# A tuned one-core kernel: the second projection of six of nine blocks as seven products of quarters, in a new order of steps

## The chip, the core and the metric

The kernel runs on one core of a Trainium2 chip. A core has five engines that work side by side, each through its own instructions in order: TensorE (PE in the rows, with its weight loads as PEld) multiplies matrices into PSUM, VectorE (DVE), ScalarE (ACT) and GpSimd (POOL) do elementwise work, and SyncE (SP) starts most transfers between DRAM and SBUF. DVE and ACT read PSUM; all of them read SBUF.

The metric is the device time of one execution in microseconds (us). A separate profiled execution gives the trace.

## The reference

```python
scores = (1 / sqrt(64)) * matmul(q, k.transpose(0, 1, 3, 2))       # q, k, v: (8, 8, 576, 64)
Dmat   = where(rel >= 0, gamma[:, None, None] ** rel, 0.0)         # rel = i - j, one gamma per head
x      = matmul(scores * Dmat, v).transpose(0, 2, 1, 3).reshape(4608, 512)
h      = x @ w_in                                                  # 512 -> 2048
g      = h + sin(alpha * h) ** 2 / (alpha + 1e-9)
out    = g @ w_out                                                 # 2048 -> 512
```

All inputs and the output are float32; both kernels compute with float16 operands and float32 sums in PSUM.

## The kernel before

The 4608 rows are worked in nine blocks of 512 tokens. Blocks 0 to 7 are the first 512 tokens of batches 0 to 7; block 8 gathers the last 64 tokens of all batches.

**Attention.** Each batch is computed in pieces with a running state: q, k and v are loaded and cast to f16 (line 168 with the decay factors, line 103 or 101 without), turned, and multiplied into scores (line 342). VectorE applies the decay mask while it takes them out of PSUM (line 354), PE multiplies by v (line 384), and a sum of keys times values (line 282) is carried from piece to piece (lines 311, 316, 323, 324). Between the two halves of an output stands a marker on an engine, a POOL nop or a PE drain, that orders them.

**The two projections.** For each block, `project` makes 16 units of 128 of the 2048 features: four matmuls of 512 columns into one PSUM bank `hps` (line 519). `sine` (ACT, line 527) makes the sine, `square` squares it (DVE or POOL line 538, ACT line 536), and `product` (DVE, line 543) computes `square / alpha + h` out of the bank into `gT`. With that the unit's bank is free. Then `gemm2` (line 562) multiplies `gT`, 128 tokens at a time, with `w_out`: 16 matmuls of 512 columns for each of four chunks of a block, into a bank `ops`. `finish` copies the chunk out of PSUM (lines 101, 103) and stores it in two halves (line 555).

**Weights.** `w_in` and `w_out` come in four pieces each on POOL's queue (lines 91 and 94), each piece of `w_out` holding 512 of the 2048 features.

**What sets the order.** Each engine takes its instructions in the order in which the program was written. For blocks 0 to 2 each step is written out by hand. For blocks 3 to 8 two loops write them: in block n, unit u is projected while one quarter (four matmuls) of a chunk of block n - 1 goes through `gemm2`, and the attention of batch n + 1 is put in at fixed units. After the last unit four chunks of block 8 remain, the last in two column pieces of 320 and 192, whose results leave on the queues of SP and ACT. Buffers are taken from pools of tiles, each kind with its own number of buffers, and PSUM banks by turns (`h0`, `h1`, `h2`, `m0`, `m1`, `op`).

## Time and profile before

| | us |
| --- | --- |
| time, median of three runs | 308.1 (308.0 to 308.36) |
| the profiled execution: span from first to last instruction | 309.4 |
| last matmul ends, in the trace | 305.78 |

Times in the trace are counted from the first instruction of the profiled execution. Its mean granted TensorE clock is 0.976: it is lower in the first 25 us only.

```profile
PE   6669999999999999999999999999999999999995
DVE  1596799989859888666866586576656746655600
ACT  1434983766544766675677567756774456555411
POOL 5690774589449587759149722990030000000000
```

Each row is an engine, each digit the busy share of one fortieth of the span (7.7 us) in tenths, 9 being 90% or more. PE is full from the fourth slice to the last but one. DVE is at 8 or 9 in most slices of the first third and at 5 or 6 later. POOL, which casts inputs and keeps the states, has nothing left in the last quarter.

### The profile page before, as it was taken

The page shows a single profiled execution, that of the slowest core. Times are in us where ns is not written, and L with a number is a line of the kernel's source. Part 1 is how long each engine was busy: PE and PEld are TensorE (multiplying, and loading weights), DVE is VectorE, ACT ScalarE, POOL GpSimd, SP SyncE. Part 2 cuts the span into 40 slices and gives each one's busy share as a digit, 9 for nine tenths or more (in the row PEclk, how much of TensorE's full clock was granted, in tenths as well). Part 3 has the DMA queues.
Part 4 walks back from the last instruction along what each step waited for, and adds up shares of the span by engine and source line. Part 5 has one row for each costly group of instructions (what it writes and reads, how often), then busy time and mean ns, then how long its engine had stood idle before and what let it go on. Part 6 is the DMA issues. An engine that isn't in the chain of part 4 may idle for free.

```text
span 309.4 us, 7922 instructions
## 1 busy us (share of the span) xinstructions
PE 296.4 (96%) x3257; PEld 150.9 (49%) x3257; DVE 207.4 (67%) x298; ACT 180.7 (58%) x286; POOL 138.4 (45%) x154
## 2 busy tenths in 40 slices
PE   6669999999999999999999999999999999999995
PEld 4546555554544544454445444544454454444443
DVE  1596799989859888666866586576656746655600
ACT  1434983766544766675677567756774456555411
POOL 5690774589449587759149722990030000000000
PEclk9776999999999999999999999999999999999999
DMA  7999999699497788987788788885431111111132
GB/s 227 335 215 217 278 260 247 160 247 303 90 289 213 88 190 183 272 140 171 161 226 209 179 163 192 230 199 132 101 72 39 34 36 36 35 34 37 42 89 73
DMA packets 115540, 49.84 MB, mean 161 GB/s; under 512 B 69792, under 2 KB 111024, under 8 KB 115504
## 3 DMA queue, kind: packets, MB, share of 16 engines
q1 hardware_dynamic: 110912, 44.97, 60.0%
q0 software_dynamic: 4224, 4.19, 8.1%
q8 instruction: 25, 0.41, 0.6%
q10 hardware_dynamic: 368, 0.18, 0.3%
q14 instruction: 11, 0.09, 0.1%
HBM read 36.74 MB, written 9.44 MB: 149 GB/s over the span
## 4 chain that ended last, share of the span: by engine, by line
PE 84%; DMA 3%; POOL 3%; SPq 3%; DVE 2%; ACT 1%; issue 1%; DVEq 0%; ACTq 0%; POOLq 0%
PE ops L562 39%; PE hps L519 37%; DMA q<-in_q_dram 3%; PE o L384 3%; PE sc L342 2%; SPq L115 2%; POOL q L168 1%; PE kv L282 1%; DVE s L316 1%; DVE ret L354 1%; PE o L406 1%; SPq L120 1%; ACT s_t L527 1%; POOL k L168 1%; PE tr L201 0%
## 5 line engine op out<-in xcount | busy, mean ns | idle before, releaser
L562 PE MATMUL ops<-w_out,gT 128*128 128x512 f16 (+2 forms) x592 | 142.4, 374 | 0.3 <-ACT kvs L101 0.2
L543 DVE SCALAR_TENSOR_TENSOR gT<-ss_t,inva,hps 128x512 f16<-128x512 f16 x144 | 106.2, 745 | 53.1 <-ACT ss_t L536 46.1
L527 ACT ACTIVATE s_t<-hps,alpha_t 128x512 f16<-128x512 f32 x144 | 97.1, 686 | 71.3 <-PE hps L519 68.8
L519 PE MATMUL hps<-xT,w_in 128*128 128x512 f16 (+1 forms) x544 | 127.7, 370 | 0.0
L519 PEld LDWEIGHTS <-w_in 128*128 128x128 f16 x608 | 59.1, 99 | 64.5 <-issue 0.9
L562 PEld LDWEIGHTS <-gT 128*128 128x128 f16 x592 | 56.2, 98 | 64.3 <-issue 0.7
L538 DVE TENSOR_TENSOR ss_t<-s_t 128x512 f16<-128x512 f16 x72 | 42.2, 587 | 19.5 <-ACT s_t L527 18.8
L536 ACT ACTIVATE ss_t<-s_t 128x512 f16<-128x512 f16 x62 | 38.8, 631 | 0.9
L354 DVE TENSOR_TENSOR ret<-sc,mask 128x1024 f16<-128x1024 f32 (+1 forms) x32 | 35.1, 1118 | 1.9 <-PE sc L342 1.8
L168 POOL TENSOR_TENSOR k<-k,cn 128x1024 f16<-128x1024 f32 (+1 forms) x13 | 22.1, 1699 | 25.0 <-DMA k<-in_k_dram 20.7
L101 ACT COPY osb<-ops 128x512 f32<-128x512 f32 (+1 forms) x34 | 19.7, 582 | 22.0 <-PE ops L562 20.6
L168 POOL TENSOR_TENSOR q<-q,cn 128x1024 f16<-128x1024 f32 (+1 forms) x16 | 27.2, 1708 | 10.1 <-DMA q<-in_q_dram 10.0
L538 POOL TENSOR_TENSOR ss_t<-s_t 128x512 f16<-128x512 f16 x10 | 10.8, 1083 | 19.5 <-ACT s_t L527 10.7
L101 ACT CAST xT<-o 128x1024 f16<-128x1024 f32 (+1 forms) x14 | 13.2, 958 | 7.9 <-PE o L406 7.8
L324 POOL TENSOR_TENSOR kvs<-s,kvs 128x256 f32<-128x256 f32 x22 | 16.1, 730 | 3.1 <-ACT kvs L101 1.4
L103 POOL CAST v<-v 128x1024 f16<-128x1024 f32 (+1 forms) x10 | 12.2, 1234 | 9.5 <-DMA v<-in_v_dram 8.4
L519 PE MATMUL hps<-xS,w_in 128*128 128x512 f16 x64 | 16.4, 379 | 0.0
L323 POOL TENSOR_TENSOR s<-kvs,cn 128x256 f32<-128x256 f32 x22 | 14.3, 651 | 0.3
L152 POOL TENSOR_TENSOR ks<-ks,cn 128x512 f16<-128x512 f32 x4 | 4.2, 1041 | 22.0 <-PE o L384 22.0
L384 PE MATMUL o<-ret,v 64*64 64x128 f16 (+1 forms) x512 | 11.9, 226 | 1.3 <-DVE ret L354 0.7
L342 PE MATMUL sc<-qT,kT 64*64 64x128 f16 (+1 forms) x512 | 10.9, 221 | 1.9 <-DVE ret L354 1.9
L316 POOL TENSOR_TENSOR s<-kvs,cn 128x256 f16<-128x256 f32 x19 | 12.2, 646 | 1.1 <-ACT kvs L101 0.5
(59 smaller groups left out, 142.3 us busy)
## 6 DMA issues: line engine op xcount, KB each, us to landing
out_dram<-osb SPq DMA_DIRECT2D x70, 128.0 KB, 2.4
q<-in_q_dram SPq DMA_DIRECT2D x16, 512.0 KB, 6.2
k<-in_k_dram SPq DMA_DIRECT2D x10, 512.0 KB, 8.2
v<-in_v_dram SPq DMA_DIRECT2D x10, 512.0 KB, 6.2
k<-in_k_dram SPq DMA_DIRECT2D x24, 128.0 KB, 3.1
v<-in_v_dram SPq DMA_DIRECT2D x24, 128.0 KB, 3.2
w_in<-in_moe_w_in_dram POOLq DMA_DIRECT2D x4, 512.0 KB, 11.3
w_out<-in_moe_w_out_dram POOLq DMA_DIRECT2D x4, 512.0 KB, 9.8
```

Of the source, the lines that this page charges most:

```text
L101: eng.copy(d_, s_)
L168: eng.tensor_tensor(dst[:, a0:a1].rearrange("p a r t d -> p t (a r) d"), t_.rearrange("p (t a) x -> p t a x", t=2)[:, :, a0:a1].rearrange( ...
L324: nc.gpsimd.tensor_tensor(self.kvs[:, c], s32, self.kvs[:, c], ADD)
L342: matmul(sc[halves(g), t, c : c + n], kT[halves(t), 2 * a + r, halves(g)], qT[halves(t), 2 * a : 2 * a + 2, 64 * g + i0 : 64 * g + 64], st ...
L354: nc.vector.tensor_tensor(ret.rearrange("p t (z x) -> p (t z) x", z=2)[:, :, 0:n], sc.rearrange("p t (z x) -> p (t z) x", z=2)[:, :, 0:n], ...
L384: made.append(matmul(o[t][halves(e), c : c + 128].rearrange("p (r i) -> p r i", r=2)[:, :, i0:64], v16[halves(g), 4 * t + 2 * x + e, r, :] ...
L519: matmul(hps_of[n, fc][0][:, cols], w_in16[:, a, fc * P : (fc + 1) * P], xs[n][:, a, cols], start=(a == 0 and part != 1), stop=(a == KT - ...
L527: nc.scalar.activation(s_t, hps, mybir.ActivationFunctionType.Sin, bias=0.0, scale=alpha_t[:, fc : fc + 1],)
L536: nc.scalar.activation(ss_t, s_t, mybir.ActivationFunctionType.Square)
L538: eng.tensor_tensor(ss_t, s_t, s_t, MULT)
L543: nc.vector.scalar_tensor_tensor(gT[n][:, fc, :], ss_t, inva[:, fc : fc + 1], hps, MULT, ADD)
L562: matmul(ops[n, c, cols.start][:, cols], gT[n][:, fk, c * P : (c + 1) * P], w_out16[:, fk, cols], start=(fk == 0), stop=(fk == FC - 1), sk ...
```

## The change

Blocks 0, 1 and 2 keep their second projection. For blocks 3 to 8 it is computed in another way. The result of a block, 512 tokens by 512 columns, is a product of `g` (512 by 2048) and `w_out` (2048 by 512). Cut both into quarters, `g` into halves of the tokens and of the features (A11, A12, A21, A22), `w_out` into halves of the features and of the columns (B11 to B22). Four quarters of the result are then sums of eight products of quarters. The change gets them from seven (the scheme of Winograd):

- four differences of the weights, made once (`TT`, line 844): T1 = B12 - B11, T2 = B22 - T1, T3 = B22 - B12 (in place of B12), T4 = B21 - T2, in eight pieces of 128 x 1024 elements;
- four sums of `g` in every block (`SM`, line 856): S1 = A21 + A22 (in place of A21), S2 = S1 - A11, S3 = A11 - A21, S4 = A12 - S2 (in place of A12), in two pieces each, 30 of the 48 pieces on DVE and 18 on POOL;
- seven products (`PP`, line 873), each of 8 units x 2 token halves, 16 matmuls of 256 columns, 112 for a block where 64 of 512 columns were; they add up in three banks, X (P1, then P6, P7, P4), Y (P2) and Z (P5, then P3);
- the banks are copied out in between (`CP`, 17 times on ACT and 7 on DVE) and added to what was copied before (`AD`, line 889, 18 times, on DVE);
- each quarter of the result is stored with two transfers from SP's queue (`OQ`, lines 894 and 895).

A piece covers 512 features, as a transfer of `w_out` does: the first of T1 reads the first quarter of `w_out`, the second the second, and the pieces of T2 to T4 the third or the fourth. T3 is made after the last use of the old B12 by block 2.

The hand-written sequence and the loops are replaced by a table `STEPS` of all steps in order, with the number of the buffer or bank that a step takes. Blocks 0 and 1 have the old order, with the pieces of T1, T2 and T4 put in; from block 2 on the order is new, block by block overlapping. Squares move as well: DVE 43 (72 before), ACT 74 (62), POOL 27 (10). The buffers are shared: 16 f32 tiles of 128 x 1024 (`r4`), 28 f16 of 128 x 1024 (`h2`), 16 f16 of 128 x 512 (`s1`), two for `g` and eight banks, any step taking a free one.

```diff
-        for n in range(3, NBLK):
...
-                    gemm2(n - 1, u, "op")
-                    finish(n - 1, u // 4)
...
-        for c in range(3):
-            tag = next(h)
-            for u in range(4 * c, 4 * c + 4):
-                gemm2(NBLK - 1, u, tag)
-            finish(NBLK - 1, c)
-        for cols, eng in ((slice(0, 320), A_), (slice(320, 512), V)):
-            tag = next(h)
-            for u in range(12, 16):
-                gemm2(NBLK - 1, u, tag, cols)
-            finish(NBLK - 1, 3, eng, cols, (nc.sync, nc.scalar))
+STEPS = """
...
+PR.0.7.2 hps.0.7=7; ST.0.3:G; SI.0.6 s.0.6=9; WO.2; TT.1.0:V T1=0; SQ.0.11:A ss.0.11=10; SI.0.7 s.0.7=11
...
+OQ.7.21; PP.8.7.1; PP.7.3.3; CP.8.7:A u3.8=27; PP.8.5.0; AD.7.12; PP.8.4.0; AD.8.22; PP.8.4.1; OQ.7.12; PP.8.4.3
+SM.8.4.1:V; PP.8.4.2; PP.8.3.3; OQ.8.22; CP.8.4:V c21.8=2; PP.8.3.1; PP.8.3.2; PP.8.3.0; OQ.8.21; AD.8.12; OQ.8.12
+"""
...
+    def quarter_a(n, t, f, i, m):
+        return g_of(n)[:, 8 * f + i : 8 * f + i + m, 256 * t : 256 * t + 256]
+    def quarter_b(f, d, i, m):
+        return w_out16[:, 8 * f + i : 8 * f + i + m, 256 * d : 256 * d + 256]
+    def of_units(x, i, m):
+        return x.rearrange("p (u n) -> p u n", n=256)[:, i : i + m]
+    def TT(t, i, eng):
+        i *= 4
+        T = {x: of_units(big16(f"T{x}"), i, 4) for x in (1, 2, 4) if f"T{x}" in place}
+        T[3] = quarter_b(0, 1, i, 4)
+        a, b = {
+            1: lambda: (quarter_b(0, 1, i, 4), quarter_b(0, 0, i, 4)),
+            2: lambda: (quarter_b(1, 1, i, 4), T[1]),
+            3: lambda: (quarter_b(1, 1, i, 4), T[3]),
+            4: lambda: (quarter_b(1, 0, i, 4), T[2]),
+        }[t]()
+        return eng.tensor_tensor(T[t], a, b, SUB)
+    def SM(n, s, i, eng):
+        i *= 4
+        S = {x: of_units(big16(f"S{x}.{n}"), i, 4) for x in (2, 3) if f"S{x}.{n}" in place}
+        S[1], S[4] = quarter_a(n, 1, 0, i, 4), quarter_a(n, 0, 1, i, 4)
+        a, b, op = {
+            1: lambda: (S[1], quarter_a(n, 1, 1, i, 4), ADD),
+            2: lambda: (S[1], quarter_a(n, 0, 0, i, 4), SUB),
+            3: lambda: (quarter_a(n, 0, 0, i, 4), S[1], SUB),
+            4: lambda: (S[4], S[2], SUB),
+        }[s]()
+        return eng.tensor_tensor(S[s], a, b, op)
+    BANK_OF = {1: "X", 6: "X", 7: "X", 4: "X", 2: "Y", 5: "Z", 3: "Z"}
+    def PP(n, p, j):
+        ps = bank(f"{BANK_OF[p]}.{n}")
+        for u in (2 * j, 2 * j + 1):
+            left, right = {
+                1: lambda: (quarter_a(n, 0, 0, u, 1), quarter_b(0, 0, u, 1)),
+                2: lambda: (quarter_a(n, 0, 1, u, 1), quarter_b(1, 0, u, 1)),
+                3: lambda: (quarter_a(n, 0, 1, u, 1), quarter_b(1, 1, u, 1)),
+                4: lambda: (quarter_a(n, 1, 1, u, 1), of_units(big16("T4"), u, 1)),
+                5: lambda: (quarter_a(n, 1, 0, u, 1), of_units(big16("T1"), u, 1)),
+                6: lambda: (of_units(big16(f"S2.{n}"), u, 1), of_units(big16("T2"), u, 1)),
+                7: lambda: (of_units(big16(f"S3.{n}"), u, 1), quarter_b(0, 1, u, 1)),
+            }[p]()
+            for c in range(2):
+                i = matmul(
+                    ps[:, 256 * c : 256 * c + 256], left[:, 0, 128 * c : 128 * c + 128], right[:, 0, :],
+                    start=starts(f"{BANK_OF[p]}.{n}"), stop=True, skip_group_check=True,
+                )
+        return i
+    KEPT = {2: ("Y", "p2"), 6: ("X", "u2"), 7: ("X", "u3"), 4: ("X", "c21")}
+    def CP(n, p, eng):
+        b, t = KEPT[p]
+        return copy(eng, mid32(f"{t}.{n}"), bank(f"{b}.{n}"))
+    SUMS = {11: ("X", "p2"), 22: ("Z", "u3"), 12: ("Z", "u2")}
+    def AD(n, c):
+        b, t = SUMS[c]
+        return nc.vector.tensor_tensor(mid32(f"{t}.{n}"), bank(f"{b}.{n}"), mid32(f"{t}.{n}"), ADD)
+    def OQ(n, c, eng=nc.sync):
+        t = mid32(f"{dict(((11, 'p2'), (21, 'c21'), (22, 'u3'), (12, 'u2')))[c]}.{n}").rearrange("p (c d) -> p c d", c=2)
+        x = rows_of(n, 2 * (c // 10 - 1), 2)[..., 256 * (c % 10 - 1) : 256 * (c % 10)]
+        eng.dma_start(x[0], t[halves(0)])
+        return eng.dma_start(x[1], t[halves(1)])
```

In the table `:V`, `:A`, `:G` and `:P` name the engine; SQ is `square`, PD `product`, PR `project`, SI `sine`, G2 `gemm2`. The names in the rows below: `r_67` are the f32 buffers, `h_68` and `s_69` the f16 ones, `g_70` the two tiles of `g`.

The first place is on DVE, in the products of block 0's first units. Before:

```order
L543 SCALAR_TENSOR_TENSOR gT<-ss_t,inva,hps 128x512
L311 SCALAR_TENSOR_TENSOR kvs<-kvs,cn,kv 128x64 x4
L543 SCALAR_TENSOR_TENSOR gT<-ss_t,inva,hps 128x512
L538 TENSOR_TENSOR ss_t<-s_t 128x512
L543 SCALAR_TENSOR_TENSOR gT<-ss_t,inva,hps 128x512 x2
```

And of the change:

```order
L792 SCALAR_TENSOR_TENSOR g_70<-s_69,inva,banks 128x512
L532 SCALAR_TENSOR_TENSOR r_67<-r_67,cn,banks 128x64 x4
L844 TENSOR_TENSOR r_67<-w_out_65 128x1024
L792 SCALAR_TENSOR_TENSOR g_70<-s_69,inva,banks 128x512
L788 TENSOR_TENSOR s_69<-s_69 128x512
L792 SCALAR_TENSOR_TENSOR g_70<-s_69,inva,banks 128x512 x2
```

The first piece of T1, which reads the first quarter of `w_out`, now stands between the state step and the product of unit 1.

The second place is on DVE too, a little later, up to the masks of batch 1 (line 354 before, 564 now). Before:

```order
L538 TENSOR_TENSOR ss_t<-s_t 128x512 x2
L543 SCALAR_TENSOR_TENSOR gT<-ss_t,inva,hps 128x512 x4
L354 TENSOR_TENSOR ret<-sc,mask 128x1024 x2
L543 SCALAR_TENSOR_TENSOR gT<-ss_t,inva,hps 128x512
L103 COPY kT<-tr 128x512 x2
L354 TENSOR_TENSOR ret<-sc,mask 128x1024 x2
```

And of the change:

```order
L788 TENSOR_TENSOR s_69<-s_69 128x512 x2
L792 SCALAR_TENSOR_TENSOR g_70<-s_69,inva,banks 128x512
L844 TENSOR_TENSOR r_67<-w_out_65 128x1024
L792 SCALAR_TENSOR_TENSOR g_70<-s_69,inva,banks 128x512 x2
L844 TENSOR_TENSOR r_67<-w_out_65,r_67 128x1024
L792 SCALAR_TENSOR_TENSOR g_70<-s_69,inva,banks 128x512
L844 TENSOR_TENSOR r_67<-w_out_65,r_67 128x1024
L564 TENSOR_TENSOR h_68<-banks,mask 128x1024 x2
```

Three more pieces stand among the last four products of block 0, ahead of the first mask of batch 1.

The third place is the end of the program on DVE. Before:

```order
L538 TENSOR_TENSOR ss_t<-s_t 128x512
L543 SCALAR_TENSOR_TENSOR gT<-ss_t,inva,hps 128x512
L538 TENSOR_TENSOR ss_t<-s_t 128x512
L543 SCALAR_TENSOR_TENSOR gT<-ss_t,inva,hps 128x512 x2
L103 COPY osb<-ops 128x192
```

And of the change:

```order
L856 TENSOR_TENSOR r_67<-g_70 128x1024
L325 COPY h_68<-banks 128x512
L856 TENSOR_TENSOR g_70<-g_70,r_67 128x4x256
L325 COPY h_68<-banks 128x512
L889 TENSOR_TENSOR h_68<-banks,h_68 128x512 x2
L856 TENSOR_TENSOR g_70<-g_70,r_67 128x4x256
L325 COPY h_68<-banks 128x512
L889 TENSOR_TENSOR h_68<-banks,h_68 128x512
```

Where squares and products of block 8 and one copy of 192 columns stood last, there are now the sums of quarters of block 8, copies and additions; the last is an addition of 512 columns.

1643 lines of the change are left out of this document (642 added, 1001 removed).

## The prediction

> **What bounds the kernel now.** I read the busy shares on the page first, then the stretches of the run side by side, then the chain of waits.
>
> ```profile
> PE 296.4 (96%) x3257; PEld 150.9 (49%) x3257; DVE 207.4 (67%) x298; ACT 180.7 (58%) x286; POOL 138.4 (45%) x154
> PE 84%; DMA 3%; POOL 3%; SPq 3%; DVE 2%; ACT 1%; issue 1%; DVEq 0%; ACTq 0%; POOLq 0%
> ```
>
> ```profile
> 0.00:25.40 25.40, 16.74 (x328) 12.85 (x329) 14.83 (x17) 7.42 (x10) 17.51 (x29) 0.79 1.06 255
> 25.40:66.00 40.60, 40.26 (x498) 22.19 (x495) 34.83 (x60) 27.90 (x46) 22.09 (x20) 0.96 1.07 241
> 66.00:105.50 39.50, 39.31 (x580) 20.12 (x572) 33.00 (x43) 23.08 (x38) 30.13 (x34) 1.00 0.76 203
> 54.40:305.80 251.40, 250.96 (x2573) 122.01 (x2571) 167.87 (x236) 153.12 (x244) 105.26 (x109) 1.00 0.61 142
> 36.00:46.00 10.00, 9.76 (x119) 5.59 (x118) 9.61 (x16) 8.68 (x16) 7.98 (x7) 1.00 1.18 252
> 66.00:76.00 10.00, 10.00 (x105) 5.37 (x98) 9.59 (x13) 6.74 (x13) 9.69 (x14) 1.00 1.00 266
> ```
>
> Columns of the second fence: stretch, its length, then busy time of PE, PEld, DVE, ACT and POOL with their counts, granted clock, DMA share, GB/s. From 25.4 us on TensorE (PE) hardly ever stops: 40.26 of 40.60, 39.31 of 39.50, and 250.96 of 251.40 from 54.4 to its last matmul. So a us of PE work removed there is a us of time, as long as nothing else makes PE wait. The same rows say how much of the others PE tolerates: with VectorE (DVE) busy for 84 to 86% it loses 0.2 to 0.34 us in 40, and even ten-us stretches with DVE at 9.6 cost it 0 to 0.24 us.
>
> **The PE work that goes.** Blocks 3 to 8 drop 6 x 64 = 384 matmuls of 512 columns for 6 x 112 = 672 of 256.
>
> ```profile
> 120.87 1.02 PE L562 MATMUL ops<-w_out,gT 128*128 128x512 f16 x4
> 121.73 1.03 PE L519 MATMUL hps<-xT,w_in 128*128 128x512 f16 x4
> 122.60 1.03 PE L562 MATMUL ops<-w_out,gT 128*128 128x512 f16 x4
> 125.19 1.03 PE L519 MATMUL hps<-xT,w_in 128*128 128x512 f16 x4
> ```
>
> ```profile
> 54.38:55.25 0.87, 0.87 (x8) 0.78 (x8) 1.00 0.02 5
> L519 PE MATMUL hps<-xT,w_in 128*128 128x256 f16 x8 | 1.0, 273 | 0.0
> ```
>
> Durations overlap, so I take start to start: from 120.87 to 125.19 five groups of four, 4.32 us for 20, 0.216 us each. Eight of 256 columns fill 0.87 us with eight weight loads beside them, 0.109 us each: half the columns, half the time, the load hidden. 384 x 0.216 = 82.9 us goes, 672 x 0.109 = 73.2 us comes: **-9.7 us**. The other matmuls stay in number. Two more PE drains between the halves of an attention product (eight instead of six) I leave inside the third term.
>
> **The wait that comes at the start.** Blocks 0 and 1 keep their order, but the weight differences T1, T2, T4 go in between, and the first piece of T1 (line 844) stands on DVE ahead of unit 1's product of block 0. DVE takes its instructions in order, and this piece reads the first quarter of w_out.
>
> ```profile
> L94 POOL DMA_DIRECT2D w_out<-in_moe_w_out_dram x1: 803/803/803, 20.8 to 20.8; - x1
> DMA to landing us min/median/max: 13.9/13.9/13.9
> ...
> DMA to landing us min/median/max: 8.6/9.8/13.9
> ```
>
> ```profile
> 29.66 0.85 DVE L311 SCALAR_TENSOR_TENSOR kvs<-kvs,cn,kv 128x64 f32<-128x64 f32 x4
> 30.43 0.74 DVE L543 SCALAR_TENSOR_TENSOR gT<-ss_t,inva,hps 128x512 f16<-128x512 f16 x1
> 33.41 0.75 DVE L543 SCALAR_TENSOR_TENSOR gT<-ss_t,inva,hps 128x512 f16<-128x512 f16 x1 [1.12 <-POOL ss_t L538]
> 34.88 0.43 DVE L538 TENSOR_TENSOR ss_t<-s_t 128x512 f16<-128x512 f16 x1 [0.39 <-ACT s_t L527]
> 39.66 1.41 DVE L543 SCALAR_TENSOR_TENSOR gT<-ss_t,inva,hps 128x512 f16<-128x512 f16 x2 [0.34 <-ACT ss_t L536]
> 48.81 2.36 DVE L354 TENSOR_TENSOR ret<-sc,mask 128x1024 f16<-128x1024 f32 x2 [0.47 <-PE sc L342]
> ```
>
> ```profile
> 32.89 6.22 PE L519 MATMUL hps<-xT,w_in 128*128 128x512 f16 x32
> 51.00 1.38 PE L384 MATMUL o<-ret,v 64*64 64x128 f16 x64
> ```
>
> The first two rows are the first quarter alone, the last is all four. The quarter lands at 20.8 + 13.9 = 34.7 us. The transfers ahead of it are the same ones in the same order, so I keep that time. DVE reaches the piece at 30.43 (where the product of unit 1 starts now) and stands until 34.7: 4.27 us. Queued behind it: products 1, 0, 3, 6, 11 of block 0, and with them PSUM banks. Unit 5's matmuls need unit 1's bank; eight matmuls after 32.89, at 34.62, PE wants it, and product 1 now ends near 36.1, 1.5 us late; unit 12 waits for the bank of unit 6 in turn. Until 51.17, where the last mask of block 1 ends (48.81 + 2.36), DVE has only 1.12 + 0.39 + 0.34 + 0.47 = 2.3 us of idle time to give back. Three more pieces stand in that stretch.
>
> What a piece costs: two f16 inputs of 1024 elements from SBUF. Nearest rows:
>
> ```profile
> L538 DVE TENSOR_TENSOR ss_t<-s_t x72: 411/426/1677, 28.1 to 290.1; 128x512 f16<-128x512 f16 x72
> L538 DVE TENSOR_TENSOR ss_t<-s_t 128x512 f16<-128x512 f16 x72 | 42.2, 587 | 19.5 <-ACT s_t L527 18.8
> L103 DVE COPY osb<-ops x3: 358/678/678, 57.2 to 305.9; 128x512 f32<-128x512 f32 x2, 128x192 f32<-128x192 f32 x1
> L354 DVE TENSOR_TENSOR ret<-sc,mask 128x1024 f16<-128x1024 f32 x20 | 23.7, 1218 | 1.9 <-PE sc L342 1.8
> L354 DVE TENSOR_TENSOR ret<-sc,mask 128x768 f16<-128x768 f32 x12 | 11.4, 951 | 0.0
> L538 POOL TENSOR_TENSOR ss_t<-s_t 128x512 f16<-128x512 f16 x10 | 10.8, 1083 | 19.5 <-ACT s_t L527 10.7
> ```
>
> 256 elements more cost the mask 0.27 us, so 0.16 us of it is fixed; the square does 512 in 0.43, twice that pace. 1024 at the square's pace: 0.16 + 0.53 = 0.69 us; bounds 0.43 (as for 512) and 1.22 (the mask's). I take 0.69, since type and memories are the square's. Back to back DVE starts the next about 0.08 us before the end (two masks take 2.36, not 2.44), so four pieces add 4 x 0.61 = 2.4. DVE late at 51.17: 4.27 + 2.4 - 2.3 = 4.4 us. PE's first product of that mask stands at 51.00 in a run of 64 without a pause, so nothing covers it, and PE is late by the same. Pieces five and six behind it may add a little: **+4.5 us**. From below 1.4 (pieces at 0.35 apart, quarter 2 us sooner), from above 7 (pieces at 1.14 apart).
>
> **The elementwise work that comes.** Counted in the list of steps, against the rows on the page: squares on DVE 43 instead of 72 (at 0.587 mean: -17.0); 30 sums of quarters at 0.69 (+20.7, up to +36.6 at 1.22); 18 additions of a bank and an SBUF tile, at 0.68 as a copy of that size (+12.2, between 0.43 and 0.75, a square and a product); copies out of PSUM (7 of products, 4 more of KV sums, 2 more half attention outputs and 1 more result at 0.68, 3 more whole outputs at 1.22: +13.2); 18 more state steps of 256 f32 elements at 0.16 + 0.27 (+7.7); casts and the last pieces of the weight differences (+5, an estimate from four casts at 0.68 to 1.22 and three pieces). Sum +42: after 54.4 us DVE has 167.9 + 42 = 210 us in 251.4 - 9.7 = 241.7 us, 87%, instead of 67%. POOL gets 18 sums at about 2.0 (twice 1.083, less the fixed part) and 17 squares, and gives up ten casts and 18 state steps; ACT gets 12 squares, and 17 copies of products replace the results of those blocks. By the counts both stay below 70%, beside PE. At 84 to 86% the two stretches above let PE lose 0.2 to 0.34 us in 40; over 242 us that is 1.2 to 2. I take **+2.0 us**, with 0.5 (as from 54.4 to 305.8 now) and 7 (below) as bounds.
>
> **The tail.**
>
> ```profile
> 304.79 0.99 PE L562 MATMUL ops<-w_out,gT 128*128 128x192 f16 x10
> 305.87 0.36 DVE L103 COPY osb<-ops 128x192 f32<-128x192 f32 x1 [12.01 <-PE ops L562]
> L555 SPq DMA_DIRECT2D out_dram<-osb x4: 466/466/588, 302.9 to 306.3; - x4
> out_dram<-osb SPq DMA_DIRECT2D x1, 48.0 KB, 1.8
> out_dram<-osb SPq DMA_DIRECT2D x70, 128.0 KB, 2.4
> ```
>
> Now 3.7 us pass from the last matmul (305.78) to the end: a copy of 192 columns, then its two halves leave from two queues. Afterwards an addition of 512 columns (0.68 for 0.36: +0.3), two halves in turn from SP (+0.47), 128 KB to land instead of 48 (+0.6): **+1.4 us**; bounds 0.3 (landing no longer than now) and 3.5 (SP late, below).
>
> **Sum.** -9.7 + 4.5 + 2.0 + 1.4 = -1.8 us on the profiled span of 309.4, so 307.6. The three runs have a median of 308.1, 1.3 below that span; the step from one kernel to the other carries over: **306.3 us**. What a measurement of this kernel can tell from no change is 0.2%, 0.6 us.
>
> **Rivals.**
> *The early wait costs little* (quarter earlier, or PE finds banks anyway). For it: 34.7 rests on one landing of 13.9 us, the longest of four with a median of 9.8. Against: PE has no slack from 25.4 on. Then -9.7 + 0.5 + 2.0 + 1.4: 302.3.
> *DVE becomes the bound through POOL: slower.* A square lasts 0.43 in the median and up to 1.68:
>
> ```profile
> 25.00:66.00 41.00, 5.12 (x10) 4.14 (x4) 0.96 1.07 241
> 66.00:105.00 39.00, 5.86 (x7) 3.43 (x3) 1.00 0.76 203
> 250.00:291.00 41.00, 7.62 (x18) 0.00 (x0) 1.00 0.17 40
> ```
>
> These are the squares alone, DVE then POOL: 0.42 each where POOL rests (250 to 291), 0.84 where it is busy for 30 of 39 us. Now POOL rests late in the run; the change gives it sums up to block 8, beside DVE's own. From unit 10 of block 7 to unit 12 of block 8 the list gives DVE 18 products, 8 squares, 3 sums and 2 additions, 20.3 us at undisturbed lengths, and PE 20.8; 11 of them read two SBUF tiles, and at 0.41 more each that is 24.8. PE is 4 us late there: 310.3. It decides from about 0.1 us more per such step on. Against: the stretch from 66 to 76 had DVE and POOL at 9.6 and PE at 10.
> The Trainium skill (SBUF — State Buffer, section "Who interferes with whom") says that a VectorE instruction with two SBUF inputs and a GpSimd one that reads SBUF hold the shared ports for their whole length, and that the later one stands until the earlier ends. The trace agrees with it (0.43 against 1.68 us). By that rule alone three sums of 2 us on POOL in that stretch could each hold DVE for up to 2 us, which would make 312.
> *The stores bind at the end.* Ten quarter results, 20 issues at 0.47 to 0.59 us, stand on SP in the last 12 us of PE work; if SP lags, the last store waits 2 us: 308.4, no difference.
> *The products don't run at half time* (weight load 98 of 109 ns): at 0.16 us each +34. The rows of 54.38 speak against it.
>
> **How the numbers follow.** My sum 0.56 (own range 304 to 308.6), little early wait 0.18, DVE bound 0.16, stores 0.08, products 0.02. Faster than 307.5: 0.46 of mine, 0.18 and 0.01 make 0.65; slower than 308.7: 0.03, 0.13, 0.02, 0.02 make 0.20; between 0.15. Range 302 to 309.8.
>
> **What would show it.** Early wait: DVE idle before line 844 until about 34.7 us, PE idle before units 5 and 12 of block 0, block 1's first product near 58.9 instead of 54.4. Half price: line 873 at 0.109 apart. DVE share near 87% with PE losing 2 us after that; if line 856 has a mean near 1.1 on DVE and PE idles before lines 770 and 873, the second rival is right. Tail: 5 us from the last matmul to the end. I am wrong if PE idles by under 1 us between 30 and 55 us, or by over 5 us later.

## The result, and the profile after

The changed kernel takes 328.08 us (median of four runs, 327.7 to 329.25); the kernel before, on the same chip beside it, 308.05 us (307.18 to 308.36). The ratio is 1.063 (interval 1.056 to 1.069): **slower by 20 us**, where 306.3 was forecast. Ratios and their intervals, here and below, leave out the executions that are over 1.5% above the fastest of the same kernel; medians are of all. The profiled execution of the change has a span of 326.4 us for a run of 328.12.

The page's slices of the changed kernel, 8.2 us each, and the granted clock in them:

```profile
PE   6876597999693899999999999999999999999993
PEclk9799597999797899999999999999999999999998
```

The loss has a place: PE has 3 to 8 in slices 4, 5, 7, 11, 13 and 14 where the page of before has 9, and its clock falls to 5 in the fifth and to 7 in the seventh, eleventh and thirteenth. From the fifteenth slice on it is full up to the last. The stretches say it in microseconds (stretch, length, then busy time of PE, PEld, DVE, ACT and POOL, granted clock, DMA share, GB/s):

```profile
25.00:66.00 41.00, 31.73 (x364) 17.10 (x364) 29.82 (x50) 20.71 (x34) 17.52 (x18) 0.88 0.89 196
66.00:105.00 39.00, 30.68 (x409) 14.96 (x409) 29.59 (x40) 18.21 (x30) 20.57 (x21) 0.91 1.04 240
105.00:145.00 40.00, 38.67 (x355) 17.78 (x354) 28.75 (x41) 21.43 (x35) 17.22 (x17) 0.96 0.65 145
145.00:185.00 40.00, 39.80 (x469) 22.66 (x468) 35.83 (x47) 21.97 (x36) 28.96 (x25) 1.00 0.74 172
185.00:225.00 40.00, 39.87 (x553) 25.89 (x550) 33.09 (x50) 29.96 (x49) 30.04 (x22) 1.00 0.63 133
225.00:265.00 40.00, 40.00 (x524) 26.31 (x523) 35.97 (x53) 22.38 (x37) 24.21 (x22) 1.00 0.37 74
265.00:305.00 40.00, 39.69 (x377) 25.06 (x375) 31.44 (x49) 28.12 (x48) 14.27 (x8) 1.00 0.23 56
36.00:40.00 4.00, 4.00 (x10) 1.40 (x10) 3.93 (x8) 1.62 (x3) 0.00 (x0) 0.50 1.20 216
100.00:104.00 4.00, 1.04 (x4) 0.30 (x4) 0.60 (x1) 0.00 (x0) 3.21 (x4) 0.71 1.19 241
104.00:108.00 4.00, 3.93 (x24) 1.67 (x25) 0.00 (x0) 0.00 (x0) 0.00 (x0) 0.50 0.79 188
```

Two things cost PE time here: it stands idle, and behind each longer stop its clock is low, so that what it does takes up to twice as long (ten matmuls of 512 columns in the 4 us from 36). I count both: idle time as the length less the busy time, and the slow clock as busy time times what is missing from 1.00.

| stretch | idle | slow clock | together |
| --- | --- | --- | --- |
| 25 to 66 us | 9.3 | 31.73 x 0.12 = 3.8 | 13.1 |
| 66 to 145 us | 8.32 + 1.33 | 30.68 x 0.09 + 38.67 x 0.04 = 4.31 | 14.0 |
| 145 to 305 us | 0.6 | 0 | 0.6 |

27.7 us are lost this way. A control below (e6b), with the order of before, loses 0.9 us from 25 to 145 us.

**The early wait.** DVE, then PE, in order of time (start, length, and in brackets the idle time ahead and what ended it):

```profile
24.83 0.85 DVE L532 SCALAR_TENSOR_TENSOR r<-r,cn,banks 128x64 f32<-128x64 f32 x4
34.57 0.69 DVE L844 TENSOR_TENSOR r<-w_out 128x1024 f16<-128x1024 f16 x1 [8.89 <-DMA w_out<-in_moe_w_out_dram]
```

```profile
35.97 6.59 PE L769 MATMUL banks<-r,w_in 128*128 128x512 f16 x24 [6.08 <-DVE g L792]
84.81 0.64 PE L551 MATMUL banks<-h 64*64 64x128 f16 x16 [2.54 <-DVE h L325]
100.00 1.04 PE L808 MATMUL banks<-w_out,g 128*128 128x512 f16 x4 [2.33 <-DVE g L792]
104.07 0.64 PE L551 MATMUL banks<-h 64*64 64x128 f16 x16 [3.03 <-DMA h<-h]
```

The piece of T1 starts at 34.57; 34.7 was forecast. But DVE is ready for it at 25.7, not at 30.43, and stands for 8.89 us. PE goes on while it has free banks, then stands for 6.08 us.

**Blocks 2 and 3.** The last three rows are another matter: PE waits for a cast, a product of DVE, and a turning of keys or queries by DMA (`h<-h`). None of them reads `w_out` or a weight difference. Two other casts stand as the piece of T1 does, one of values on ACT and one of keys on DVE, each for a load:

```profile
87.97 1.04 ACT L325 CAST h<-r 128x1024 f16<-128x1024 f32 x1 [7.05 <-DMA r<-in_v_dram]
109.58 1.22 DVE L448 TENSOR_TENSOR h<-r,cn 128x1024 f16<-128x1024 f32 x1 [8.98 <-DMA r<-in_k_dram]
```

The chain of waits that leads to the second runs along SP's queue: turnings, loads and a store one after another from 92.5 to 104.7 us, and behind them these keys, which are issued at 104.7 and land at 109.56.

**The tail**: 4.9 us from the last matmul (321.5) to the end (326.4), 5 were forecast.

```profile
321.54 0.69 DVE L889 TENSOR_TENSOR h<-banks,h 128x512 f32<-128x512 f32 x1 [1.06 <-PE banks L873]
322.37 0.59 SPq L894 DMA_DIRECT2D out_dram<-h  x1
```

SP starts to send the last quarter 0.14 us after its addition ends (322.23): SP's queue does not lag.

### The profile page after: what moved, and what is told of

It reads as the page before. It is cut to its first block, busy times and chain, and to the rows that moved or that the text cites. A ratio compares the mean times of both kernels' runs of the same rounds, so it can differ in the third digit from the quotient of the medians.

```text
span 326.4 us, 8503 instructions
## 1 busy us (share of the span) xinstructions
PE 295.2 (90%) x3529; PEld 177.4 (54%) x3529; DVE 250.5 (77%) x365; ACT 176.9 (54%) x285; POOL 173.8 (53%) x162
## 4 chain that ended last, share of the span: by engine, by line
PE 64%; DVE 15%; DMA 8%; SPq 4%; POOL 3%; issue 2%; ACT 2%; ACTq 0%; DVEq 0%
PE banks L769 31%; PE banks L873 21%; PE banks L808 6%; DVE g L792 5%; DMA w_out<-in_moe_w_out_dram 4%; DVE s L788 2%; SPq L480 2%; PE banks L551 2%; PE banks L582 2%; DMA r<-in_q_dram 2%; DVE h L564 2%; DMA r<-in_k_dram 1%; DVE h L448 1%; DVE r L844 1%; SPq L425 1%
## 5 line engine op out<-in xcount | busy, mean ns | idle before, releaser
L769 PE MATMUL banks<-r,w_in 128*128 128x512 f16 (+1 forms) x608 | 142.5, 376 | 7.7 <-DVE g L792 6.8
L777 ACT ACTIVATE s<-banks,alpha 128x512 f16<-128x512 f32 x144 | 94.7, 686 | 80.2 <-PE banks L769 76.4
L792 DVE SCALAR_TENSOR_TENSOR g<-s,inva,banks 128x512 f16<-128x512 f16 x144 | 102.8, 741 | 17.8 <-ACT s L787 15.1
L788 POOL TENSOR_TENSOR s<-s 128x512 f16<-128x512 f16 x27 | 28.8, 1071 | 59.6 <-ACT s L777 58.4
L448 POOL TENSOR_TENSOR h<-r,cn 128x1024 f16<-128x1024 f32 (+1 forms) x26 | 44.4, 1715 | 22.7 <-PE banks L769 13.9
L873 PEld LDWEIGHTS <-g 128*128 128x128 f16 x480 | 46.1, 98 | 12.7 <-POOL g L856 0.3
L808 PE MATMUL banks<-w_out,g 128*128 128x512 f16 x192 | 48.8, 394 | 2.3 <-DVE g L792 2.3
L787 ACT ACTIVATE s<-s 128x512 f16<-128x512 f16 x74 | 45.8, 630 | 1.6 <-DMA s<-s 0.2
L873 PE MATMUL banks<-w_out,g 128*128 128x256 f16 x288 | 37.7, 273 | 0.0
L564 DVE TENSOR_TENSOR h<-banks,mask 128x1024 f16<-128x1024 f32 (+1 forms) x32 | 35.1, 1117 | 2.9 <-PE banks L551 2.3
L808 PEld LDWEIGHTS <-g 128*128 128x128 f16 x192 | 18.2, 101 | 25.0 <-issue 3.2
L873 PEld LDWEIGHTS <-r 128*128 128x128 f16 x192 | 18.6, 98 | 4.7 <-issue 0.4
L527 POOL TENSOR_TENSOR r<-h,r 128x256 f32<-128x256 f32 x15 | 11.8, 788 | 9.5 <-ACT r L325 4.2
## 6 DMA issues: line engine op xcount, KB each, us to landing
w_in<-in_moe_w_in_dram POOLq DMA_DIRECT2D x4, 512.0 KB, 11.8
w_out<-in_moe_w_out_dram POOLq DMA_DIRECT2D x4, 512.0 KB, 11.1
```

The lines of the kernel that those rows point to most:

```text
L448: return eng.tensor_tensor(dst[:, a0:a1].rearrange("p a r t d -> p t (a r) d"), t_.rearrange("p (t a) x -> p t a x", t=2)[:, :, a0:a1].rea ...
L564: return nc.vector.tensor_tensor(ret(b, p, y).rearrange("p t (z x) -> p (t z) x", z=2)[:, :, 0:n], bank(f"sc.{b}.{p}.{y}", 2).rearrange("p ...
L769: i = matmul(bank(hps)[:, cols], w_in16[:, a, u * P : (u + 1) * P], x_of(n)[:, a, cols], start=starts(hps), stop=(a == KT - 1), skip_group ...
L777: return nc.scalar.activation(small(f"s.{name}")[:, cols], bank(f"hps.{name}")[:, cols], mybir.ActivationFunctionType.Sin, bias=0.0, scale ...
L787: return nc.scalar.activation(ss_t, s_t, mybir.ActivationFunctionType.Square)
L788: return eng.tensor_tensor(ss_t, s_t, s_t, MULT)
```

## The experiments

Two theories stood at the outset: **the early wait**, its price with all that follows, makes up the loss, or **the new order** from block 2 on loses time by itself. (A third, that the products or DVE's sums cost PE time, is already spoken against by the stretches from 145 us on.) Every kernel is compared with the kernel before as run beside it on the same chip. Those medians went from 307.7 to 310.9 us, so ratios count, not times taken on different chips.

### e4: the kernel before with one piece of T1

```diff
+        gT[1] = work.tile([P, FC, 512], F16, tag="gT", bufs=2, name="gT")
+        nc.vector.tensor_tensor(
+            gT[1][:, 0:2].rearrange("p a (b c) -> p (a b) c", b=2),
+            w_out16[:, 0:4, 256:512], w_out16[:, 0:4, 0:256], mybir.AluOpType.subtract,
+        )
```

The piece stands ahead of the product of unit 1 of block 0; nothing uses its result.

> The kernel before with one instruction added: the first piece of T1 on VectorE ahead of unit 1's product of block 0, its result not used. It shows the wait alone in the old order. By the prediction's term the piece waits from 30.4 to 34.7 us and TensorE loses about 4 us: 312 us. If the wait sets off a convoy of late casts, transposes and loads in the old order as well, more than 316 us. If TensorE finds its banks anyway, 308 to 309 us.

Measured: 318.6 us, 1.035 (1.031 to 1.039), **+10.9 us** from one instruction of 0.69 us. DVE, PE and a stretch:

```profile
34.79 0.69 DVE L714 TENSOR_TENSOR gT<-w_out 128x1024 f16<-128x1024 f16 x1 [8.22 <-DMA w_out<-in_moe_w_out_dram]
```

```profile
36.20 1.01 PE L201 MATMUL tr<-ident,q 128*128 128x128 f16 x8 [8.11 <-DVE gT L543]
```

```profile
36.00:40.00 4.00, 3.80 (x16) 1.94 (x16) 2.58 (x6) 2.22 (x4) 0.00 (x0) 0.54 1.19 216
```

PE idles 8.11 us, and the clock of 0.54 in the 4 us behind it takes 3.80 x 0.46 = 1.7 more: 9.8 of the 10.9. (One later stop, 1.78 us at 203.8 us, is not in the profile of before either.) So the early wait alone costs more than the products save.

### e1, e2, e5: the pieces later, in the new order

e1 moves the first piece behind 48 other steps, beside the second:

```diff
-... WO.2; TT.1.0:V T1=0; SQ.0.11:A ss.0.11=10; ...
+... WO.2; SQ.0.11:A ss.0.11=10; ...
-... G2.0.1.0 op.0.1=6; TT.1.1:V
+... G2.0.1.0 op.0.1=6; TT.1.0:V T1=0; TT.1.1:V
```

> The changed kernel with one step moved: the first piece of T1 stands beside its second piece on VectorE, 48 steps later, when its quarter of w_out has landed. Theory W (the wait): the time lost before 160 us hangs on VectorE's 8.9 us wait; late casts hold the transposes on SP's queue, and the loads behind them come late. Then the 6.1 us stall of TensorE at 36 us goes, block 1 starts near 54 instead of 61.9, and the stalls between 80 and 116 us shrink to less than half: about 314 us. Theory O (the order): the order of blocks 2 and 3 stalls by itself. Then only the first stall and the slow clock behind it go, about 8 us: 320 us, with the stalls between 80 and 116 us as they are (over 8 us).

e2 moves all six early pieces of T1, T2 and T4 into block 3:

```diff
-... WO.2; TT.1.0:V T1=0; SQ.0.11:A ss.0.11=10; ...
+... WO.2; SQ.0.11:A ss.0.11=10; ...
+... PD.3.1 gT.3=1; TT.1.0:V T1=0; SQ.3.2:A ss.3.2=6; ... PD.3.0; TT.1.1:V; ...
```

> The changed kernel with all six pieces of T1, T2 and T4 moved behind the first products of block 3 on VectorE, ahead of any use. W: TensorE idles for less than 3 us between 25 and 120 us, and the kernel comes to 302 to 306 us, faster than before. O: the stalls between 80 and 116 us stay, 316 to 319 us, slower than before.

e5 is e2 with eight loads for batches 5 and 6 and block 8 moved down SP's queue, behind the turning of batch 4's keys:

```diff
-SC.2.1.0 sc.2.1.0=6; OS.0.1; LE.0.k rs.0.k=8; ST.2.0:G s16.2=26; OS.0.0; ST.2.3:V; LD.5.k.1 raw.5.k.1=3
+SC.2.1.0 sc.2.1.0=6; OS.0.1; ST.2.0:G s16.2=26; OS.0.0; ST.2.3:V; ...
+... XP.4.k.0 kT.4.0=23; LD.5.k.1 raw.5.k.1=3; LD.5.q.1 raw.5.q.1=13; LE.0.k rs.0.k=8; ...
```

> The second experiment's kernel with eight loads (two of batch 5, one of batch 6, five of the last rows) moved on SP's queue from ahead of the transposes of batch 3 to behind the first transpose of batch 4. Theory S (SP's queue is full from 57 to 105 us, and these loads keep the transposes and the keys of batch 4 waiting): the transposes of batch 3 leave 7 to 9 us sooner, TensorE's stalls near 90, 94 and 105 us (6.6 us, and some 3 us of slow clock behind them) go, and the kernel takes 313 to 316 us instead of 323.4. Theory D (VectorE is late there and the banks with it): the stalls stay, 321 to 324 us.

Measured: e1 323.2 us in the median of two runs 6 us apart (320.3 and 326.1), e2 323.4 us, 1.050 (1.046 to 1.053), e5 319.7 us, 1.031 (1.022 to 1.040). Without the early wait **only 4 to 5 us come back** (by ratio and by median), where e4 had it at 10.9. The stretches say why. From 25 to 66 us e2 loses 2.4 us where the change loses 13.1, so the wait is gone with its price. But PE stands at later places: from 66 to 105 us e2 loses 11.8 us, the change 11.1; from 125 to 145 us, where the pieces now stand, it loses 4.5, the change nothing; and e2's profiled execution starts its first projection at 24.7 us, the change's at 21.2. In all e2 loses 8.4 us less from 25 to 145 us, and its later start takes 3.5 of them. In e2, PE, a stretch and SP's queue:

```profile
75.40 0.42 PE L551 MATMUL banks<-h 64*64 64x128 f16 x16 [1.62 <-DVE h L325]
89.86 1.04 PE L808 MATMUL banks<-w_out,g 128*128 128x512 f16 x4 [2.33 <-DVE g L792]
93.83 0.64 PE L551 MATMUL banks<-h 64*64 64x128 f16 x16 [2.94 <-DMA h<-h]
```

```profile
66.00:105.00 39.00, 29.87 (x352) 14.30 (x354) 25.64 (x33) 14.63 (x24) 20.71 (x24) 0.91 1.02 234
```

```profile
85.98 2.78 SPq L421 DMA_DIRECT2D r<-in_v_dram  x4
88.81 4.56 SPq L480 DMA_TRANSPOSE h<-h  x3
```

SP hardly pauses from 57 to 105 us, and the turnings of batch 3 stand behind loads for batches 5 and 6, which nobody needs yet. e5 shows this as the cause of one stop: with eight loads out of the way the idle 2.94 us for `h<-h` at 93.83 is gone (a stop of 1.4 us for `h<-h` came at 70.8). The other two stay, now 2.6 us at 73.9 and 2.3 at 89.9 us. That moving the loads saves time on the whole is not shown: e5's time is 4 to 6 us below e2's, but from 25 to 145 us PE loses 18.8 us in e5 and 18.6 in e2, and e5's profiled execution starts its first projection 3.2 us sooner, which is most of the 4.0 us between the two spans. The second theory holds all the same: the order from block 2 on loses 11 to 12 us from 66 to 105 us without any early piece.

### e3: the new order without the products

The sums, differences, products and additions are left out; units of four matmuls of 512 columns (`GU`), each computing part of the ordinary second projection, stand where products stood.

```diff
-EKP.1.0:V x.8=1; EVB.0; PP.7.1.1; EKP.0.0:V; PR.7.5.2 hps.7.5=0; ...
+EKP.1.0:V x.8=1; EVB.0; EKP.0.0:V; PR.7.5.2 hps.7.5=0; ...
+ESC.0 sce.0=4; KP.7.0.2:V; GU.6.0.4.5.6.7; GU.6.0.8.9.10.11; ...
```

> The kernel of the second experiment's order without the seven products: no weight differences, no sums, no additions; blocks 3 to 8 multiply four chunks of 128 tokens with 512 columns again, at the places where the products P2, P1, P7 and P5 stood. It shows what the products are worth in one order. If they are worth their columns (9.7 us less on TensorE, 1.2 more at the end), this kernel is 7 to 9 us slower than the second experiment; if the elementwise work eats the gain, it is within 3 us of it or faster. W says 311 to 315 us, O says 324 to 328.

Measured: 343.2 us, 1.117 (1.111 to 1.123), 15 us above the change itself. That doesn't price the products: the place of the units makes waits of its own, 120 - 110.58 = 9.4 us of idle PE from 145 to 265 us where the change has 0.3.

```profile
145.00:265.00 120.00, 110.58 (x1200) 51.57 (x1191) 71.21 (x104) 65.97 (x106) 45.68 (x46) 0.99 0.52 113
```

Of it I keep what comes before, where the steps are the change's own less the products and pieces. The stops from 71 to 103 us stand in e3 too (five, 1.5 to 2.65 us), and the stretch loses 11.0 us idle and 2.5 by the clock:

```profile
66.00:105.00 39.00, 28.03 (x325) 12.74 (x324) 24.24 (x31) 11.74 (x18) 21.86 (x24) 0.91 1.08 240
```

This loss needs neither products nor pieces.

### e6b, e7: the old order in the new form

To separate the form of the change (a table, shared buffers) from its order, e6b writes out the order of before as such a table, with the ordinary second projection for all blocks.

```diff
-STEPS of the change (new order from block 2 on, TT, SM, PP, CP, AD, OQ)
+STEPS with every step where the kernel before has it, G2 and FI for blocks 0 to 8
```

> The kernel before written as a table, mended: each step stands behind the last use of the bank that it takes. Every engine has the order of the kernel before, blocks 0 to 8, no products; the buffers are shared as in the change and the last chunk is in one piece. If table and buffers cost nothing: 308 to 309 us. If the shared buffers make loads or copies collide: over 311 us.

Measured: 313.5 us, 1.019 (1.014 to 1.023). The stretches of e6b, and its one long stop:

```profile
25.00:66.00 41.00, 40.44 (x521) 22.62 (x519) 36.83 (x62) 29.35 (x50) 22.65 (x24) 1.00 1.17 254
66.00:105.00 39.00, 38.62 (x549) 19.13 (x548) 31.94 (x42) 22.13 (x36) 28.93 (x32) 1.00 0.83 205
105.00:145.00 40.00, 40.00 (x417) 19.20 (x415) 30.44 (x41) 26.35 (x42) 29.86 (x32) 1.00 0.85 190
```

```profile
180.34 1.02 PE L795 MATMUL banks<-w_out,g 128*128 128x512 f16 x4 [3.89 <-ACT h L312]
```

The stop of 3.89 us is a shared buffer given out too late for a result's copy; apart from it and the slow clock behind it (0.67 from 180 to 184 us and 0.91 to 188, 1.6 us) the table shows no cost, and the first 145 us are those of before. So it isn't the form. (An earlier build of this list, e6, 326.1 us, let some steps take a bank ahead of its last reader, so that sums of several blocks mixed; its time is not used.)

Side by side, PE's idle time and slow clock together, in us:

| kernel | first projection at | 25 to 66 us | 66 to 105 us | 105 to 145 us |
| --- | --- | --- | --- | --- |
| the change | 21.2 | 13.1 | 11.1 | 2.9 |
| e1, first piece later | 21.3 | 5.6 | 11.4 | 1.3 |
| e2, all pieces later | 24.7 | 2.4 | 11.8 | 4.5 |
| e5, e2 with loads later | 21.5 | 1.0 | 10.7 | 7.1 |
| e3, no pieces, no products | 21.5 | 0.9 | 13.5 | 0 |
| e6b, old order | 21.5 | 0.6 | 0.4 | 0 |

The first column of losses goes with the early pieces, the second with the order: 10.7 to 13.5 us wherever block 2 on is in the new order, 0.4 where it is in the old one. (e2's 2.4 holds 1.6 us of the slow clock of its late start, which lasts until 28 us, as in the profile of before.)

e7 puts the products into the old loops, with one pair of attention banks. It mixes such sums too, so it can tell of the waits only roughly.

> The seven products in the order of the kernel before: blocks 0 to 2 as they were there, the loops of blocks 3 to 8 with two product pieces behind a unit in place of one quarter of a chunk, one pair of banks for the attention and two banks for the products, the weight differences on VectorE during block 3. If the products are worth what the prediction made of them (9.7 us of columns, less about 2 for VectorE and about 1 at the end), 300 to 303 us, faster than before. If VectorE or the smaller number of banks becomes the bound, over 306 us.

At 344 us it was the slowest: with one pair of banks PE waits 2.2 to 3.5 us for a mask in each of three blocks, and there are other stops of up to 3.9 us. That says nothing on the products, and is inconclusive.

### e8, e9, e10: the old start, then the change, and the early pieces put back

e8 takes every step of blocks 0 to 2 as before, then the change's steps; the pieces stand where DVE is idle, after `w_out` has landed. e9 gives the steps behind the seam, the place where the old order ends and the change's steps begin, other banks, so that fewer of them wait for a bank of block 2, and moves the two pieces of T4 into block 3. In both, loads for batches 5 and 6 and block 8 stand further back, as in e5. e10 is e9 with the six pieces at the change's early places:

```diff
+TT.1.0:V
 PD.0.1
...
 PD.2.3
-TT.1.0:V
...
-TT.1.1:V
...
-TT.2.0:V; TT.2.1:V
...
```

> Blocks 0 to 2 in the order of the kernel before up to the last product of block 2, then the rest of the change's own steps in the change's order, with its seven products; the loads of the last rows and of batches 5 and 6 stand in the order of need, and the pieces of T1, T2 and T4 at places where VectorE was idle in the kernel before, after the whole of w_out has landed. If the change loses its time in the start alone (the early wait, and the order of SP's loads and of blocks 2 and 3), TensorE idles for under 3 us from 25 us on, and the kernel takes 299 to 303 us, faster than before by the products' 9.7 us less 1 to 3 us. If the order of blocks 3 to 8, or VectorE's load there, is a cause as well, over 306 us.

> The kernel of the old start followed by the change's steps, with the seam mended: there TensorE stood for 1.4 and 3.3 us at 108 to 113 us because the first units of block 3 took banks that the last units of block 2 still held. The banks of the second part are renumbered in pairs so that the first units of block 3 take free ones, and the two pieces of T4 go from the seam into block 3. If those stalls and the slow clock behind them (about 2 us) were all that kept the products' gain away: 303 to 306 us, faster than before. If TensorE meets the same wait under other numbers: 310 to 312 us.

> The kernel of the ninth experiment with the six pieces of T1, T2 and T4 put back to their places of the change in blocks 0 and 1; nothing else differs. It prices the early pieces alone: the wait of the first one for w_out (VectorE reaches it near 26 us, the quarter lands near 34.6) and the load of the others. One piece alone in the old order made the kernel before 10.9 us slower. If the five others add nothing: 9 to 12 us above the ninth; if they add their 3 us and a convoy: 13 to 18 us above it.

Measured: e8 311.4 us, 1.004 (1.000 to 1.008); e9 310.7 us, 1.007 (1.003 to 1.011); e10 322.9 us, 1.046 (1.038 to 1.054). e9 and e10 ran side by side: **the early pieces cost 12.2 us**, the same order as e4's 10.9. Their first stretches, e9 and then e10:

```profile
25.00:66.00 41.00, 40.58 (x522) 22.89 (x521) 36.85 (x62) 29.59 (x49) 23.05 (x24) 1.00 1.17 256
```

```profile
25.00:66.00 41.00, 34.30 (x380) 19.18 (x380) 31.33 (x52) 22.56 (x37) 17.48 (x18) 0.91 0.80 179
```

The idle time differs by 6.3 us and the slow clock adds 3.1 more, 9.4 of the 12.2; e10's profiled execution also starts its first projection 3.1 us later. There the piece waits 4.65 us and starts at 34.30: the landing does not move, so a late start shortens the wait by what it has itself cost before.

And **the old start, without early pieces, does not yet make it faster**. The products themselves are worth most of what was forecast. From block 4's first projection to the end of the run e6b takes 174.0 us (137.0 to 311.0), e9 160.8 (146.2 to 307.0); the projections of blocks 4 to 8 and the same attention products lie in both. e6b, then e9:

```profile
137.00:311.00 174.00, 165.59 (x1481) 77.54 (x1479) 97.06 (x140) 97.38 (x156) 44.19 (x45) 0.99 0.47 109
```

```profile
146.20:307.00 160.80, 155.33 (x1761) 103.70 (x1759) 129.07 (x193) 94.41 (x155) 87.68 (x66) 1.00 0.49 105
```

Of the 13.2 us between them 3.9 are e6b's stop and 1.6 the slow clock behind it, and 0.9 are eight of e9's 672 matmuls of products, which came earlier. That leaves 6.8 us, tail included; on PE alone it is 165.59 - 1.6 against 155.33 + 0.9, **7.8 us where 9.7 was forecast**. What takes the other 1.9 us I did not follow.

But at 146.2 e9 is already 9 us behind e6b, with stops at the seam. The times of e8 and e9 are those that I had expected if the order of blocks 3 to 8 (e8) or the same bank wait under other numbers (e9) were a cause. The traces put the loss at the seam: from 105 to 125 us PE is busy for 15.35 of 20 us in e8 and 15.90 in e9, from 145 to 185 us for 39.25 and 39.83 of 40. The longest stop there changed its place and length from e8 to e9, 3.29 us at 112.9 and 2.66 at 122.2, and a shorter one near 109 stayed, 1.36 and 1.43 us. ACT and PE in e9:

```profile
115.85 1.04 ACT L324 CAST h<-r 128x1024 f16<-128x1024 f32 x1 [6.55 <-DMA r<-in_v_dram]
```

```profile
122.19 4.00 PE L807 MATMUL banks<-w_out,g 128*128 128x512 f16 x11 [2.66 <-DVE g L791]
```

A cast of values on ACT waits 6.55 us for its load. Queued behind it are sines of block 3, behind those the products on DVE, and PE waits for `g`. It is the early wait again: one instruction that waits for a transfer, on an engine that takes its work in order.

### e11, e12, e13: the waits at the seam, one after another

```diff
 e11, from e9:
-CA.5.v.0.2:A          (cast of batch 5's values, at the head of the seam)
+CA.5.v.0.2:A          (behind FI.2.2)
 e12, from e11:
-CA.6.q.0.2:V          (behind SI.3.15)
+CA.6.q.0.2:V          (behind PD.3.14)
 e13, from e12:
-LD.6.q.0              (behind TT.3.0)
+LD.6.q.0              (ahead of LD.6.k.1)
-XP.5.k.1              (behind PR.4.9)
+XP.5.k.1              (ahead of LD.7.v.1)
```

e11 also lets two quarters of a chunk of block 2 go ahead of two units of block 3.

> The ninth experiment's kernel with the seam mended again: a cast of batch 5 on ScalarE, which waited for its load from 109 to 116 us while the sines of block 3 stood behind it, goes behind a later copy, and the first four PE steps after block 2 change places, so that a unit with a free bank comes first. If these two waits (4.1 us of idle TensorE at 109 and 122 us, and some 2 us of slow clock behind them) are what keeps the products' 9.7 us from the end: a span of 300 to 302 us in the profile, a median of 302 to 305 us, faster than before. If the order of blocks 3 to 8 or VectorE's load there costs by itself: 307 to 310 us.

> The kernel is e11 with one step moved: VectorE's cast of batch 6's first query rows (CA.6.q.0.2:V), which in e11 waited 2.31 us for its transfer at 145.7 us with the last two products of block 3 queued behind it, now stands behind the product of unit 14 of block 3 (PD.3.14). Theory A, the gain of 9.7 us on TensorE is whole and only in-order waits at the seam between blocks 2 and 4 hide it: TensorE's idle 2.41 us at 148.4 goes, the granted clock of 0.84 from 150 to 160 us (1.6 us of a full clock) is 1.00, so 4.0 us off e11: span near 302, median near 305.7, ratio to the kernel before 0.98 to 0.99. Theory B, one wait is followed by the next one (the transfers of batch 6 are late on SP's queue, so that its scores or masks wait instead): some 0 to 1.5 us off, median 308 to 309.7, with an idle time of TensorE over 1 us between 150 and 185 us.

> The kernel is e12 with two steps moved on SP's queue: the load of batch 6's first query rows (LD.6.q.0), which landed at 147.8 us in e12's profile behind rows that are wanted later, now stands ahead of batch 6's second keys (LD.6.k.1), 6 transfers and some 5.7 us sooner; and the turning of batch 5's second keys (XP.5.k.1, 155.9 us) stands ahead of four transfers of batch 7's values, 2.7 us sooner. Theory A (the seam's waits are late transfers and can be mended one by one): VectorE's wait of 2.35 us at 147.8, TensorE's idle 2.55 and 0.97 us at 150.7 and 154.4 and 2.57 us at 161.8 go, some 4 to 6 us off e12's profiled span, ratio to the kernel before 0.975 to 0.985. Theory B (the next transfer is late in turn): idle time of TensorE of over 4 us in all stays between 145 and 180 us, ratio as e12's, 0.985 to 0.995.

| kernel | median | before beside it | ratio (interval) |
| --- | --- | --- | --- |
| e9 | 310.7 | 308.4 | 1.007 (1.003 to 1.011) |
| e11 | 309.7 | 310.7 | 0.999 (0.995 to 1.004) |
| e12 | 308.4 | 310.1 | 0.989 (0.980 to 0.998) |
| e13 | 309.1 | 310.7 | 0.985 (0.977 to 0.993) |

The ratio of e12 rests on four of its seven runs, that of e13 on two of twelve. By the medians of all runs both are 0.5% faster than before; by the means e13 is 1.7 us faster (0.2 to 3.2) and e12 1.6 (from 4.2 faster to 1.0 slower). So e13 beats the change by far, and the kernel before by some 0.5%, which is close to the noise; 1.5% is not shown.

In e11 the stop for the cast of values went, and the next stood at 145 us. DVE, then PE:

```profile
145.72 1.23 DVE L447 TENSOR_TENSOR h<-r,cn 128x1024 f16<-128x1024 f32 x1 [2.31 <-DMA r<-in_q_dram]
```

```profile
148.44 1.02 PE L768 MATMUL banks<-r,w_in 128*128 128x512 f16 x4 [2.41 <-DVE g L791]
```

e12 moves that cast behind two products. In its profile the load is later too, and the wait has only other products behind it; a turning is late in turn:

```profile
147.79 1.22 DVE L447 TENSOR_TENSOR h<-r,cn 128x1024 f16<-128x1024 f32 x1 [2.35 <-DMA r<-in_q_dram]
```

```profile
161.79 0.37 PE L550 MATMUL banks<-h 64*64 64x128 f16 x16 [2.57 <-DMA h<-h]
```

So e12's theory A (the one cast is the rest) fell in the profile. (These are profiles of one execution each, and e12's took 313.0 us, where its median is 308.4: how much of its stops is usual stays open.) e13 moves what is late, the load and the turning, up SP's queue, and both stops go. What is left of PE's stops over 0.5 us there in e13:

```profile
168.69 0.37 PE L582 MATMUL banks<-h 64*64 64x128 f16 x16 [0.66 <-DVE h L564]
170.67 1.89 PE L769 MATMUL banks<-r,w_in 128*128 128x512 f16 x8 [1.07 <-DVE g L792]
```

Idle time and slow clock from 140 to 180 us of those profiles: 2.6 + 1.5 us in e11, 7.4 + 1.3 in e12, 2.6 and a full clock in e13. Against e11, then, e13's profile gains the slow clock alone there. What is gained over the kernel before stays under the 6.8 us that the products leave after tail and additions; where the rest goes in e13 I did not follow further.

## Why the prediction was wrong

**Where the time went**, against the steps of the sum:

| term | forecast | measured |
| --- | --- | --- |
| products for matmuls | -9.7 | -7.8 on PE (e9 against e6b) |
| early wait | +4.5 | +10.9 (e4), +12.2 (e10 less e9), 13.1 in the change's first stretch |
| DVE's extra work | +2.0 | 0.6 us of idle PE from 145 to 305 us |
| tail | +1.4 | 4.9 us for 3.7: +1.2 |
| order from block 2 on | 0 | 14.0 in the change's stretches from 66 to 145 us, 13.5 in e3's |

With -7.8, 13.1, 14.0, 0.6 and 1.2 less the 0.9 that the control loses too, the sum is +20.2 us, for 20.0 between the medians. The spans agree less well: the change's 326.4 stands 20.9 us above e6b's without its stop and the slow clock behind it (305.5). With e6b's tail of 4.5 us the sum is 19.4 there, and 1.5 us are not placed.

**The step "the wait that comes at the start" was mis-sized, in two ways.** The place and the mechanism were right: the landing (34.57 us for 34.7), the products queued behind, the banks. The first error is DVE's arrival. I took 30.43 us from the one profiled execution of before, whose first projection starts at 25.4 us. In the change's it starts at 21.2, and in the profiles of e1, e3 to e5, e6b, e8, e9, e11 and e12 at 21.3 to 22.4 (in those of e2, e10 and e13 at 24.7 to 25.4). The landing doesn't move with it: 34.57 us in the change, 34.79 in e4. So the 4 us by which DVE was late anyway belong to that execution, and against the usual ones the wait is 8.9 us, not 4.3. That same execution hid in the last step: its span of 309.4 is above the median of the runs of 308.1, though a run holds more than a span; the change's has 326.4 in a run of 328.12. The "1.3 below that span" that I carried over was the sign that it was not a typical one.

The second error is that no term stood for the clock. Behind a stop of 6.08 us PE's granted clock is 0.50 for 4 us, behind 8.11 us in e4 0.54; behind the two stops of 2.33 and 3.03 us that end at 100.00 and 104.07 us it is 0.71 from 100 to 104 and 0.50 from 104 to 108. The Trainium skill has the rule (TensorE: Matmul & The Clock Gate, section "What's actually happening"): half rate after an idle window of some 3.4 us, full rate after a busy one of that length. The stops of 6 and 8 us agree with it, and so such a stop costs PE about 2 us beyond its length (2.0 and 1.7 us in those 4 us). The two short ones show that less than a whole idle window can be enough. I had read the low clock of the first 25 us on the page and not asked what a new stop would do. Together, the 4.5 us of the term, 4.6 for DVE's arrival and 2 for the clock make 11.1, between the 10.9 of e4 and the 12.2 of e10 less e9.

**The new order from block 2 on had no term at all.** I counted what each engine has to do and took the order as good wherever no new wait was in sight. Yet the order also moved loads on SP's queue ahead of the turnings that blocks 2 and 3 wait for, and put casts that wait for their loads ahead of sines and products. It cost more than any term of the sum. That it is the order is shown: e3 has it without pieces and products and loses 13.5 us from 66 to 105 us, e2 and e5 without early pieces 11.8 and 10.7, and e6b in the old order 0.4. Which of the change's stops from 84 to 114 us is due to which load was shown only for the turning that e5 freed. For the rest, e9 to e13 show the pattern, one waiting instruction after another, and not the single cause.

**What was right.** Products of 256 columns at half the time of 512; two rows of the change:

```profile
315.22 1.91 PE L873 MATMUL banks<-w_out,r 128*128 128x256 f16 x16
316.97 0.60 PE L873 MATMUL banks<-w_out,g 128*128 128x256 f16 x4
```

16 in 1.75 us are 0.109 each, as taken, though over whole blocks the gain is 1.9 us smaller than forecast. The rival of 0.16 us falls, and so does that of the stores.

**The slower rival was the wrong one.** DVE as the bound through POOL was, apart from 0.02 for the products, the only case that would have made the kernel slower. Its conditions came: sums on DVE have a mean of up to 0.94 us for 0.69, on POOL 2.1 to 2.2 for 2.0.

```profile
L856 POOL TENSOR_TENSOR r<-g 128x1024 f16<-128x1024 f16 x11 | 24.1, 2190 | 21.7 <-PE banks L705 12.4 <-DVE g L792 4.5 <-DVE g L856 4.3
L856 DVE TENSOR_TENSOR r<-g 128x1024 f16<-128x1024 f16 x13 | 12.2, 941 | 0.1
```

But PE hardly feels them: DVE is busy for 33 to 36 us of 40 from 145 to 265 us, and PE loses 0 to 0.2 in each 40. Of the stated signs, the first (DVE idle before line 844, PE idle behind) came true at twice its size (8.89 us for 4.27; block 1's first projection stands at 61.9 us for 58.9 forecast, and at 49.6 in e6b); the last, "over 5 us later", did too, and that one was named as what would make the prediction wrong.
